# Attention into channel mixing on one core: values, differences and mixes in stretches of 512 columns

## The chip, the cores and the metric

One NeuronCore of a Trainium2 chip runs the whole program. The metric is device time in microseconds for one launch. Engines are named as in the profile: PE (TensorE's matmuls), PEld (its weight loads), DVE (VectorE), ACT (ScalarE), POOL (GpSimd), SP (SyncE). POOL issues the input loads, SP and ACT the stores.

## The reference, cut to what matters

There are 8 batches of 8 heads, 576 tokens, head dimension 64 and 32 memory slots. The model width is 8 x 64 = 512, the hidden width 1024.

```
a    = softmax(phi, axis=tokens)              # per batch, head and memory slot
k_m  = a.T @ k ;  v_m = a.T @ v               # 32 x 64 per head
x    = softmax(q @ k_m.T / 8) @ v_m           # 576 x 64 per head, heads side by side: 576 x 512
prev = x shifted by one token (zero first)
xk   = mu_k * x + (1 - mu_k) * prev
xr   = mu_r * x + (1 - mu_r) * prev
out  = sigmoid(xr @ w_r) * (relu(xk @ w_k)**2 @ w_v)
```

## The kernel before, in words

Everything between the loads and the stores stays on the chip, in bf16 with f32 accumulation. Tokens are the columns. A batch's 576 columns are nine blocks of 64 (QR): column 64 j + p holds token 9 p + j. The previous token of a column is therefore 64 columns to the left, except in block 0, where it is the last block, one column back.

The work is a list of steps, written out by hand as words in PLAN, and run in that order. Each step issues its instructions at once; each engine works through its own instructions strictly in the order of the plan, and waits only for the data and buffers that an instruction needs. PSUM has 8 banks; BANKS says which bank each new PSUM tile takes. The words used below:

- `b:exp`, `b:k`, `b:v`, `b:ko`, `b:kov`: exponential of phi (L255, ACT); matmul groups over the tokens that give keys, values and sums of the memory slots (L269, tile kvps). `b:zk`, `b:nk`/`b:ak`, `b:nv`/`b:av`: reciprocal of the sums; keys and values scaled, on DVE or ACT. `b:tk`/`b:ta`: transposing the keys.
- `b:q0`, `b:q1`: transposing q on DVE (L353). `b:s`: scores on PE and their exponentials on ACT (L368, L373).
- `b:fe`, `fs`, `fo` and `qe`, `qs`, `qo`: the softmax sums, folded and unfolded on DVE (L400 to L419). `b:y`, `b:w`: weights, exponential by reciprocal sum (L428, tile atn).
- `b:x0`, `b:x1`: the values of a batch, in its first 320 and its last 256 columns: 8 matmuls (L322, tile nops) and four copies from PSUM to the tile x (L440), all on ACT, or shared with DVE if the word ends in m.
- `b:d0d`, `b:d2d`: differences x - prev for two of the four 128-row parts (L452, L453). Three subtractions: two over whole blocks, one of 63 columns for block 0, and a copy for the first column.
- `b:k0d`, `b:r2e`, ...: mixes. The difference is scaled by mu - 1 (tile mu_d; on DVE at L465 if the word ends in d, on ACT at L463 if in e), and x added to it (L466), into xkT or xrT. These are rings of 4 batches (2304 columns).
- `c0:...` to `c8:...`: keys: 128 of 1024 hidden rows, times a stretch of columns: 4 matmuls (L576), the relu on ACT (L580), the square on DVE (L588), or on ACT if the word ends in s (L586). Stretch 0 is batch 0; stretches 1 to 8 have 512 columns each (the last 448), starting at column 576.
- `g:t`: the gate of 128 tokens: 4 matmuls (L609) and a tanh on ACT (L612). `o:t`: the product with w_v: 8 matmuls (L626), and the gating on DVE (L628), then the stores on SP.
- `0:mk`, `0:mr`: batch 0 alone mixes mu into v_m first (`nk`, `nr`: L474, tile vm), and lets the matmuls give xk and xr (L322, tile mxps, copied at L491).
- `busyNxM`: N matmuls of M x 128 columns on zeros (L214, tile idle). `p:...`: the loads on POOL's queue, of phi, k, v, q and the weights, each into one of two buffers.

Of the kernel before, what the change touches and what calls it, by code (L numbers as in the profile page):

```python
# [60 lines left out]
def kernel(  # L61
# [175 lines left out]

    def attention(b):
        st = {}
# [78 lines left out]
        def head_tiles(pss, src, lo, hi, cols=slice(0, None), **flags):  # L318
            for c in range(2):
                for g in range(HH):  # L320
                    r = slice(g * M, (g + 1) * M)
                    nc.tensor.matmul(pss[g][c * D:(c + 1) * D, cols], lhsT=src[r, c], rhs=st["at"][r, c, lo:hi],  # L322
                                     skip_group_check=True, **flags)
# [107 lines left out]
        def values(hf, both=False):  # L431

            def go():
                if "x" not in st:
                    st["x"] = own([128, ND, S], BF16, "x", 3)
                sl = HALVES[hf]
# [250 lines left out]
```

## Time and profile before

| | |
|---|---|
| three runs | 201.19, 201.27, 203.62 us; median 201.27 |
| profiled execution | 201.65 us, of which the span is 199.9 us |
| PE busy | 191.9 us (96%) |
| DVE busy | 151.3 us (76%) |
| ACT busy | 144.5 us (72%) |
| chain that ended last | PE 91%, ACT 4%, DVE 2% |
| DMA, mean over the span | 157 GB/s |
| TensorE's granted clock | 1.0 in all slices |

The span is the time from the first to the last recorded instruction; what the profiled execution took beyond it lies around it. Busy times of one group of instructions can be less than count times mean, since neighbours overlap. A line of the chain gives the start, the length and what ran; a line of a group gives count, busy time and mean, and then the idle time of the engine before it.

### The profile page before, as it was taken

Reading aid. Unit: us, or ns where it says so; the run is one execution under the profiler, and the core shown is the slowest. Engines: PE = TensorE matmul, PEld = TensorE weight load, DVE = VectorE, ACT = ScalarE, POOL = GpSimd, SP = SyncE. Lnnn points to the kernel's source line nnn. Section 1 sums busy time; section 2 is a strip of 40 time slices with the busy share of each in tenths; the row PEclk is TensorE's granted clock in tenths of the full one; section 3 lists DMA queues with packets and bytes.
Section 4 is the critical chain, followed back from the end, with each engine's and each line's share of the span. In section 5 each row is a group of like instructions: output and inputs, shape, how many; then the busy total and the mean of one; then the engine's idle time right before and its main releaser. Section 6 shows DMA issues by size and latency. Waiting matters only on the chain.

```text
span 199.9 us, 5381 instructions
## 1 busy us (share of the span) xinstructions
PE 191.9 (96%) x2148; PEld 99.6 (50%) x2170; DVE 151.3 (76%) x401; ACT 144.5 (72%) x311; POOL 29.7 (15%) x45
## 2 busy tenths in 40 slices
PE   8997999899999999999999999999999999999992
PEld 3474755585445445454457544444344444444451
DVE  5049698998689999999999999999997950031231
ACT  2236979648899998999799997876759868933210
POOL 7743142200143004070200000000000000000000
PEclk9999999999999999999999999999999999999999
DMA  6999999999999999999999421322422015014553
GB/s 160 191 261 209 205 208 198 268 214 293 233 218 230 286 259 281 206 240 224 207 253 190 106 56 35 71 54 54 99 62 52 2 41 119 0 38 101 116 117 105
DMA packets 24522, 31.30 MB, mean 157 GB/s; under 512 B 1960, under 2 KB 19632, under 8 KB 24496
## 3 DMA queue, kind: packets, MB, share of 16 engines
q0 software_dynamic: 17392, 20.91, 56.2%
q1 hardware_dynamic: 6336, 9.18, 18.4%
q10 hardware_dynamic: 768, 0.85, 1.3%
q8 instruction: 17, 0.28, 0.5%
q14 instruction: 9, 0.07, 0.1%
HBM read 38.28 MB, written 9.44 MB: 239 GB/s over the span
## 4 chain that ended last, share of the span: by engine, by line
PE 91%; ACT 4%; DVE 2%; issue 1%
PE pv L626 32%; PE pk L576 31%; PE pr L609 14%; PE idle L214 5%; PE kvps L269 4%; PE scps L368 2%; PE nops L322 2%; ACT sg L612 1%; PE mxps L322 1%; ACT e L373 1%; ACT L612 1%; DVE atn L428 1%; ACT rl L580 1%; PE ktps L335 1%; DVE lz L419 0%
## 5 line engine op out<-in xcount | busy, mean ns | idle before, releaser
L576 PE MATMUL pk<-xkT,wk 128*128 128x512 bf16 (+4 forms) x344 | 67.2, 340 | 0.4
L626 PE MATMUL pv<-wv,sq 128*128 128x512 bf16 (+1 forms) x320 | 65.6, 353 | 0.4
L580 ACT ACTIVATE rl<-pk 128x512 bf16<-128x512 f32 (+3 forms) x80 | 42.5, 552 | 13.1 <-PE pk L576 12.0
L576 PEld LDWEIGHTS <-wk 128*128 128x128 bf16 x352 | 33.0, 98 | 28.6 <-issue 1.4
L626 PEld LDWEIGHTS <-sq 128*128 128x128 bf16 x328 | 31.2, 98 | 29.0 <-issue 0.4
L609 PE MATMUL pr<-wr,xrT 128*128 128x512 bf16 x138 | 35.5, 380 | 0.3
L628 DVE SCALAR_TENSOR_TENSOR o<-sg,pv 128x512 f32<-128x512 f32 (+1 forms) x41 | 24.6, 615 | 13.7 <-PE pv L626 13.0
L612 ACT ACTIVATE sg<-pr 128x512 f32<-128x512 f32 x36 | 20.9, 594 | 13.6 <-PE pr L609 13.5
L588 DVE TENSOR_TENSOR sq<-rl 128x320 bf16<-128x320 bf16 (+5 forms) x55 | 15.8, 323 | 14.6 <-ACT rl L580 14.0
L586 ACT ACTIVATE sq<-rl 128x512 bf16<-128x512 bf16 (+5 forms) x49 | 24.5, 518 | 1.3
L463 ACT ACTIVATE mu_d<-diff,mu 128x576 bf16<-128x576 bf16 x30 | 21.4, 768 | 3.9 <-DVE diff L453 3.4
L609 PEld LDWEIGHTS <-xrT 128*128 128x128 bf16 x144 | 13.8, 98 | 15.6
L214 PE MATMUL idle<-zeros 128*128 128x512 bf16 (+3 forms) x74 | 13.6, 346 | 1.0 <-DVE zeros L143 1.0
L440 ACT CAST x<-nops 128x320 bf16<-128x320 f32 (+1 forms) x34 | 11.5, 420 | 2.9 <-PE nops L322 2.9
L466 DVE TENSOR_TENSOR xrT<-x,mu_d 128x1152 bf16<-128x1152 bf16 x14 | 10.5, 751 | 3.5 <-ACT mu_d L463 3.2
L428 DVE TENSOR_TENSOR atn<-e,lz 128x320 bf16<-128x320 bf16 (+2 forms) x31 | 12.9, 452 | 0.1
L452 DVE TENSOR_TENSOR diff<-x 128x512 bf16<-128x512 bf16 (+1 forms) x42 | 12.4, 352 | 0.4 <-ACT x L440 0.4
L353 DVE STREAM_TRANSPOSE qT<-q 128x576 uint32<-128x576 uint32 x16 | 11.9, 761 | 0.7 <-DMA q<-in_q_dram 0.7
L419 DVE STREAM_TRANSPOSE lz<-se 128x320 f32<-128x320 f32 (+3 forms) x21 | 11.9, 587 | 0.1
L373 ACT ACTIVATE e<-scps 128x288 bf16<-128x288 f32 x32 | 10.5, 421 | 1.7 <-PE scps L368 1.7
L255 ACT ACTIVATE em<-ph 128x1152 bf16<-128x1152 f32 (+1 forms) x9 | 9.4, 1060 | 2.6 <-DMA ph<-in_phi_dram 2.6
L410 DVE TENSOR_REDUCE se<-eT 128x18 f32<-128x576 bf16 (+3 forms) x15 | 10.9, 729 | 0.2
(68 smaller groups left out, 147.3 us busy)
## 6 DMA issues: line engine op xcount, KB each, us to landing
out_dram<-o SPq DMA_DIRECT2D x61, 128.0 KB, 2.4
...
kvs<-in_k_dram POOLq DMA_DIRECT2D x7, 576.0 KB, 16.9
q<-in_q_dram POOLq DMA_DIRECT2D x6, 576.0 KB, 12.6
...
```

The source lines that it names most:

```text
L214: nc.tensor.matmul(ps.rearrange("p (a b) -> p a b", b=128), lhsT=zeros, rhs=zeros.unsqueeze(1).to_broadcast([128, blocks, 128]), start=Tru ...
L373: nc.scalar.activation(e[:, hf], pss[c, hf], AF.Exp, scale=scale)
L428: nc.vector.tensor_mul(st["at"][:, c, sl], st["e"][:, c, sl], st["lz"][:, c, sl])
L463: nc.scalar.activation(t[:, i], st["d"][:, pr + i, :], AF.Copy, scale=mu1[:, o:o + 1])
L576: nc.tensor.matmul(pk[:, p0 - lo:p1 - lo], lhsT=wk_sb[:, di, fi * 128:(fi + 1) * 128], rhs=xk_T[:, di, p0 % RING:p0 % RING + p1 - p0], sta ...
L580: nc.scalar.activation(rl, pk, AF.Relu, scale=HALF_ROOT)
L586: nc.scalar.activation(sq[:, fi, p:p + p1 - p0], rl[:, part], AF.Square)
L588: nc.vector.tensor_mul(sq[:, fi, p:p + p1 - p0], rl[:, part], rl[:, part])
L609: nc.tensor.matmul(pr, lhsT=xr_T[:, di, c0:c0 + 128], rhs=wr_sb[:, di, :], start=(di == 0), stop=(di == ND - 1))
L612: nc.scalar.activation(gated[t], pr, AF.Tanh, scale=0.5)
L626: nc.tensor.matmul(pv[:, cols], lhsT=sq[:, fi, p:p + 128], rhs=wv_sb[:, fi, cols], start=(fi == 0), stop=(fi == NF - 1))
L628: nc.vector.scalar_tensor_tensor(o[:, cols], in0=gated[t][:, cols], scalar=1.0, in1=pv[:, cols], op0=AL.add, op1=AL.mult)
```

## The change

The steps `x0`/`x1`, `d` and `k`/`r` of batches 1 to 7 are no longer made per batch but per stretch of the 4032 columns of these batches: stretches x1 to x8, 512 columns each, the last 448. A batch's blocks are stored rotated by one: block 0 comes last in the ring (the stores take that into account), so that the mixes of a column need x at the same place and 64 columns ahead. The tile x of a stretch has 64 + 512 columns; its first 64 are copied on DVE from the tail of the stretch before.

A values step has four PSUM tiles of up to 512 columns; where a stretch contains the border of two batches, each batch's columns have their own matmuls. Only the first stretch makes its values in two pieces of 320 and 256. Differences are one subtraction over the stretch, and for a batch's end in it one of 63 columns and one copy. A mix is one addition over the stretch (two where the ring wraps), and one of 64 columns for a batch's end.

The tiles vb have four buffers instead of three. PLAN and BANKS are new throughout: words in another order, some steps by other engines (`ak` for `nk`, a key with s or without), fillers of other sizes, and loads in another order. Batch 3 takes its keys and values in two groups (`3:ko`, `3:v`).

```diff
 PLAN = [
-    "0:busy23x4 0:exp0 0:exp1 0:k0c 0:z p:k:0b p:q:00 p:q:01 0:k1c 0:busy16x3 0:ak 0:ta 0:q0 0:q1 0:mub 0:s1 0:s0",
-    "0:qe2 0:qe3 p:phi:1 p:v:0 0:busy25x1 0:fs1 0:qo2 0:qo3 1:exp 0:l0 0:v 0:h0z 0:y2 0:y3 0:l1 0:y0 0:nk0 0:nk1",
-    "0:busy10x2 0:h1z 0:y1 p:wk:4-8 0:nr1 0:mk0 0:mk1 c0:6a c0:7b p:wk:0-4 c0:5bs c0:7a c0:3bs p:k:1 0:nr0 c0:1b",
-    "c0:3a c0:2a c0:4b p:q:10 0:mr0 1:ko p:q:11 1:zk 1:nk c0:4a 1:q0 c0:6bs 1:q1 c0:1a 0:mu 1:ta 0:mr1 c0:0a 1:s0",
-    "1:s1 1:qe1 p:wr:0-4 1:qe0 1:fe1 c0:0bs p:v:1 c0:5as 1:fs0 c0:2bs 1:fs1 g:2 1:qo0 1:fo1 g:3 g:0 1:v 1:y0 1:qo1",
-    "1:y2 1:nv 1:y1 g:1 1:y3 1:x0m p:wv:0-2 1:x1m 1:d0d o:3a 1:d2d 1:k0d o:2a p:wv:2-4 o:1a 1:k2e o:0a o:3b o:1b",
-    "1:r0d p:phi:2 2:exp p:k:2 o:0b o:2b c1:3s 2:ko p:q:2 2:zk 2:ak 1:r2d c1:4s c1:6s 2:tk 2:q0 g:7 2:q1 c1:0 p:v:2",
-    "c1:5 2:s 2:qe2 2:qe3 2:qe1 2:fs1 2:qe0 2:fs0 2:qo2 2:y2 c1:7s g:6 2:fo0 2:v 2:qo3 p:phi:3 2:y0 c1:1s c1:2s g:5",
-    "2:av 2:y1 p:k:3 p:v:3 2:y3 3:exp g:4 o:5 2:x0m g:8 2:x1m 3:kov p:q:3 3:zk 2:d2d 2:d0d 3:ak 3:q1 3:av o:7 2:k2e",
-    "3:tk p:v:4 3:q0 2:k0e o:6 o:4 2:r2e 3:s 3:fe0 c2:1s 2:r0d c2:7 c2:2s 3:fe1 3:fs c2:6 p:q:4 c2:3s 3:fo0 3:fo1",
-    "p:phi:4 g:11 g:9 3:y0 p:k:4 3:y3 4:exp p:k:5 3:y1 3:y2 c2:5 p:phi:5 c2:4 c2:0 g:12 3:x1m 4:kov 3:x0m 4:zk 3:d0d",
-    "4:ak 3:d2d 4:av o:8 3:k0e 4:q1 p:phi:6 4:q0 3:k2e g:10 p:v:5 5:exp 4:tk o:10 3:r0d o:11 c3:0 5:kov p:q:5 5:zk",
-    "3:r2e 4:s c3:1s p:phi:7 4:qe0 4:qe1 4:fe1 4:fs 5:ak p:k:7 c3:3 4:qo3 c3:5 4:y3 4:fo0 5:q0 7:exp g:13 5:nv 6:exp",
-    "4:qo2 4:y1 c3:4 4:y2 5:ta c3:7 5:q1 o:9 c3:2s c3:6 4:y0 g:15 p:v:7 4:x1m o:13 4:x0 4:d0d 7:kov 5:s 7:zk1 7:zk0",
-    "4:d2d 5:qe1 5:qe0 5:qe2 7:ak 5:qe3 4:k0d 4:k2e 5:fs 5:fo 4:r0e p:q:6 o:15 o:12 6:q0 g:16 7:av c4:3s 5:y2 p:k:6",
-    "c4:2 p:q:7 g:17 c4:6s 7:q0 7:q1 4:r2e p:v:6 c4:7 7:ta c4:5 c4:4 5:w0 5:y3 g:14 c4:0 c4:1 7:s o:14 6:q1 5:x1",
-    "6:kov 6:zk 7:fe0 5:x0 7:qs0 6:nk g:20 6:av 7:fe1 g:18 5:d0d 5:r0d 5:d2d o:16 7:qs1 5:k0e 5:k2e g:19 5:r2d 7:qo0",
-    "7:qo1 6:ta o:17 7:fs1 o:18 c5:0 6:s 6:fe1 6:fe0 6:qs3 c5:2s 6:qs0 6:qo3 6:qs1 c5:3s 6:fo0 6:qs2 g:21 6:qo2 6:y1",
-    "6:y2 6:y3 c5:7s c5:5s 6:y0 c5:6 7:y0 o:19 7:qo2 c5:4s 7:y2 c5:1s g:23 g:24 7:y1 6:x1m o:23 g:22 7:qo3 6:x0m",
-    "6:d0d 7:y3 o:20 6:d2d 7:x0m 6:k0e 6:k2d o:22 7:x1m 7:d0d o:21 g:26 c6:4s c6:1s 7:d2d c6:2s 7:k0d 7:k2d c6:5s",
-    "7:r0e 6:r0d c6:3 g:25 c6:0 c6:6 c7:3 c6:7 c7:0s 6:r2d c7:1s 7:r2e c7:7s o:25 o:24 o:26 c8:6 g:27 c7:6s c8:2 g:28",
-    "c8:5s c8:3s c8:0s g:31 c7:5s c8:4 c8:1s c7:2s g:32 c7:4 o:27 o:28 c8:7s g:29 o:31 g:30 o:30 o:32 g:34 g:33 o:33",
-    "o:29 g:35 o:34 o:35",
+    "0:busy3x2 0:busy22x2 0:busy13x4 0:exp1 p:k:0b 0:exp0 0:k0c 0:mu 0:z 0:k1c p:q:01 0:ak 0:q1 0:hc0 p:q:00 0:q0",
+    "0:ht1 0:mub 0:s0 0:s1 0:qe2 0:qe3 0:busy3x1 p:v:0 0:busy3x1 0:fs1 0:l1 0:v 0:nk0 0:nr0 0:l0 0:h0z p:phi:1 0:qo2",
+    "p:wk:4-8 0:nr1 0:busy16x2 0:qo3 0:nk1 p:k:1 0:y2 0:y3 0:h1z 0:y1 0:y0 0:mk1 0:mk0 1:exp c0:4bs 0:mr1 c0:6b 1:ko",
+    "p:wk:0-4 c0:6a p:q:11 1:zk c0:5a 1:ak c0:4a c0:2a p:q:10 1:q1 c0:3b c0:7bs 1:q0 1:ta 0:mr0 c0:2b c0:5b c0:3a",
+    "1:s1 1:fe1 p:wr:0-4 1:s0 p:v:1 1:qe0 1:qe1 c0:7a c0:0a 1:fs1 1:fs0 1:qo0 1:qo1 c0:1b c0:1as g:0 c0:0bs 1:fo1",
+    "1:y2 g:2 1:v p:wv:0-2 1:y0 1:av 1:y1 g:1 1:y3 g:3 x1:v0 o:3a x1:v1m x1:d0d p:wv:2-4 x1:d2d o:2a x1:k0d p:phi:2",
+    "x1:k2d o:1a 2:exp o:1b p:k:2 o:2b x1:r0d o:3b o:0a o:0b 2:ko 2:zk0 2:zk1 p:q:2 x1:r2d 2:q0 c1:3 2:ak 2:q1 c1:5",
+    "c1:0s p:v:2 c1:1 2:tk c1:4 c1:2 2:s 2:qe0 2:v 2:qe2 c1:6s p:phi:3 g:4 g:7 2:qe3 p:k:3 2:qs2 2:qs3 2:qo2 2:qe1",
+    "p:q:3 2:qo3 2:fs0 2:fo0 3:exp 2:y3 g:6 2:y1 2:y0 c1:7s g:5 2:av 2:y2 o:7 x2:v 3:q0 3:ko 3:zk 3:ak x2:d0d x2:d2d",
+    "3:q1 x2:k0e o:6 o:4 x2:k2e 3:ta x2:r2e x2:r0d o:5 p:v:3 3:s p:phi:5 3:fe0 3:v c2:1 c2:6s p:q:4 3:fe1 3:fs 5:exp",
+    "p:phi:4 c2:2 3:qo1 p:v:5 p:v:4 c2:4s 3:nv c2:3 3:qo0 3:qo2 3:y1 3:y2 3:qo3 g:9 p:k:4 c2:0 c2:5s 3:y3 3:y0 g:8",
+    "g:11 4:q0 c2:7 g:10 4:q1 x3:v x3:d0d x3:d2d x3:k2d 4:exp x3:k0e o:11 o:8 o:10 4:kov 4:zk p:k:5 x3:r2e x3:r0e",
+    "4:ak 5:kov p:q:5 p:phi:7 4:av 5:zk0 5:zk1 5:nk c3:6 5:q0 p:v:7 c3:2 4:ta o:9 p:k:7 p:phi:6 4:s 4:qe1 4:fe1 4:qe0",
+    "c3:4 4:fs 5:q1 c3:1 4:fo0 4:qo2 c3:7 7:exp 4:qo3 5:ta 4:y2 5:av p:q:6 4:y3 p:q:7 4:y0 4:y1 g:12 g:14 c3:3 p:v:6",
+    "c3:0 c3:5 5:s 7:kov x4:v 5:qe0 5:qe2 g:15 x4:d0d x4:d2d x4:k2d x4:k0e g:13 o:13 p:k:6 7:zk0 7:zk1 5:qe3 x4:r0e",
+    "7:ak 5:qe1 o:15 x4:r2e o:12 c4:4 5:fs c4:0 c4:2 7:av c4:5 6:exp 5:fo1 c4:1s 5:fo0 7:ta c4:6s 5:y2 5:y0 o:14 g:18",
+    "x5:v 7:q1 7:q0 x5:d0d 5:y1 6:kov x5:d2d 6:zk g:19 6:q1 c4:3 7:s 6:q0 c4:7s x5:k2d 6:nv g:16 7:qe1 x5:k0e g:17",
+    "x5:r0d 7:qs1 o:18 x5:r2e 5:y3 7:qe0 o:17 7:qe2 7:qe3 6:ak c5:5 c5:7s 6:ta c5:4s 7:fs1 o:16 6:s 7:qo3 7:qs0 6:qe2",
+    "6:fe0 6:qe3 6:qs0 6:qs1 g:21 6:qs2 6:fo0 6:qo2 c5:3 7:qo0 c5:1 6:y2 6:y0 7:qo2 g:23 6:qs3 7:y2 g:22 6:y1 c5:2s",
+    "c5:0s 6:qo3 6:y3 c5:6s 7:y3 o:19 x6:v x6:d0d o:23 7:y0 x6:d2d x6:k0d x6:k2e o:22 o:21 x7:v g:20 o:20 c6:5 x7:d0d",
+    "7:qo1 x6:r0e c6:2 x6:r2d c6:3 c6:0s c6:7 x7:k0e x7:d2d c6:1s c6:4 c6:6s 7:y1 g:26 g:27 g:25 o:27 x7:k2d x7:r0e",
+    "x7:r2d x8:v x8:d0d x8:d2d o:25 o:26 c7:1 g:31 g:24 x8:r2d x8:k2e c7:0 c7:2 c7:3 c7:7s c7:5s g:30 x8:k0d o:24",
+    "c7:6s c7:4s x8:r0d g:28 c8:3 c8:4 o:28 c8:7 c8:0s o:31 c8:2 g:33 o:30 g:34 c8:6s c8:5 c8:1s g:32 g:29 o:32 o:33",
+    "g:35 o:29 o:34 o:35",
 ]
...
+    states = [{} for _ in range(B)]
+
+    def head_tiles(pss, st, src, lo, hi, cols=slice(0, None), **flags):
+        for c in range(2):
+            for g in range(HH):
+                r = slice(g * M, (g + 1) * M)
+                nc.tensor.matmul(pss[g][c * D:(c + 1) * D, cols], lhsT=src[r, c], rhs=st["at"][r, c, lo:hi],
+                                 skip_group_check=True, **flags)
+
     def attention(b):
-        st = {}
+        st = states[b]
...
-                vb = own([128, 2, D], BF16, "vb", 3)
+                vb = own([128, 2, D], BF16, "vb", 4)
...
-        def values(hf, both=False):
-        def diff(pr, n=1):
-        def mix(which, pr, n=1, by_act=False):
...
+    TOK = (B - 1) * S
+    xs, ds = {}, {}
+    def chunk_x(c):
+        lo = (c - 1) * CT
+        hi = min(lo + CT, TOK)
+        n, plain = hi - lo, min(hi, TOK - QR) - lo
+        ends = [b * S - QR for b in range(1, B) if lo <= b * S - QR < hi]
+        def tile_x():
+            if c not in xs:
+                xs[c] = work.tile([128, ND, QR + CT], BF16, name="x", tag=f"x{c % 3}")
+            return xs[c]
+        def values(c0, c1, both=False):
+            def go():
+                x = tile_x()
+                if c > 1:
+                    nc.vector.tensor_copy(x[:, :, :QR], xs[c - 1][:, :, CT:])
+                pss = [psum.tile([128, CT], F32, name="nops", tag=bank())[:, :c1 - c0] for _ in range(ND)]
+                for b in range(1, B):
+                    g0, g1 = max(lo + c0, (b - 1) * S), min(lo + c1, b * S)
+                    if g0 < g1:
+                        head_tiles(pss, states[b], states[b]["vb"], g0 - (b - 1) * S, g1 - (b - 1) * S,
+                                   slice(g0 - lo - c0, g1 - lo - c0), start=True, stop=True)
+                for i in range(ND):
+                    (nc.vector.tensor_copy if both and i % 2 else nc.scalar.copy)(x[:, i, c0:c1], pss[i])
+            return go
+        def diff(pr, m):
+            def go():
+                if c not in ds:
+                    ds[c] = work.tile([128, ND, CT], BF16, name="diff", tag=f"diff{c % 2}")
+                x, d = xs[c][:, pr:pr + m], ds[c][:, pr:pr + m]
+                nc.vector.tensor_sub(d[:, :, :plain], x[:, :, QR:QR + plain], x[:, :, :plain])
+                for e in ends:
+                    e -= lo
+                    first = xs[c - 1][:, pr:pr + m, e:e + QR]
+                    nc.vector.tensor_sub(d[:, :, e + 1:e + QR], first[:, :, 1:], x[:, :, e:e + QR - 1])
+                    nc.vector.tensor_copy(d[:, :, e:e + 1], first[:, :, :1])
+            return go
+        def mix(which, pr, m, by_act=False):
+            def go():
+                ring = (xk_T, xr_T)[which][:, pr:pr + m]
+                t = work.tile([128, 2, CT], BF16, name="mu_d", tag=turn("mu_d", 2))[:, :m]
+                for i in range(m):
+                    o = which * ND + pr + i
+                    if by_act:
+                        nc.scalar.activation(t[:, i, :n], ds[c][:, pr + i, :n], AF.Copy, scale=mu1[:, o:o + 1])
+                    else:
+                        nc.vector.tensor_scalar_mul(t[:, i, :n], ds[c][:, pr + i, :n], mu1[:, o:o + 1])
+                x = xs[c][:, pr:pr + m]
+                cut = -(S + lo) % RING
+                for p0, p1 in ((0, cut), (cut, plain)) if 0 < cut < plain else ((0, plain),):
+                    g = (S + lo + p0) % RING
+                    nc.vector.tensor_add(ring[:, :, g:g + p1 - p0], x[:, :, QR + p0:QR + p1], t[:, :, p0:p1])
+                for e in ends:
+                    e -= lo
+                    g = (S + lo + e) % RING
+                    nc.vector.tensor_add(ring[:, :, g:g + QR], xs[c - 1][:, pr:pr + m, e:e + QR], t[:, :, e:e + QR])
+            return go
+        return values, diff, mix
+    def chunk_steps(c):
+        values, diff, mix = chunk_x(c)
+        n = min(CT, TOK - QR - (c - 1) * CT)
+        spans = {"0": (0, 5 * QR), "1": (5 * QR, S)} if c == 1 else {"": (QR, QR + n)}
+        steps = {}
+        for w, (c0, c1) in spans.items():
+            steps[f"v{w}"] = values(c0, c1)
+            steps[f"v{w}m"] = values(c0, c1, True)
+        steps["dd"] = diff(0, ND)
+        for i in (0, 2):
+            steps[f"d{i}d"] = diff(i, 2)
+            for w in range(2):
+                steps[f"{'kr'[w]}{i}d"] = mix(w, i, 2)
+                steps[f"{'kr'[w]}{i}e"] = mix(w, i, 2, by_act=True)
+        return steps
...
             j, p0 = divmod(r, QR)
+            j = (j + 1) % NJ if b else j
...
+    chunks = {f"x{c}": chunk_steps(c) for c in range(1, len(STARTS))}
...
+        elif who in chunks:
+            todo.append((n, -1, word, chunks[who][name]))
```

More of the change, by code (lines that the diff above doesn't have):

```diff
@@ L316, in norm_v @@
             return go
[L318 to L323, printed above, removed]
         def reload():
@@ L429, in weigh @@
             return go
-        def values(hf, both=False):
[L433 to L436, printed above, removed]
-                pss = [half_tile(hf, "nops") for _ in range(ND)]
-                head_tiles(pss, st["vb"], sl.start, sl.stop, start=True, stop=True)
-                for i in range(ND):
-                    (nc.vector.tensor_copy if both and i % 2 else nc.scalar.copy)(st["x"][:, i, sl], pss[i])
-            return go
-        before = [[(QR, 5 * QR, 0), (1, QR, S - QR)], [(5 * QR, S, 4 * QR)]]
-        def diff(pr, n=1):
-            def go():
-                if "d" not in st:
-                    st["d"] = own([128, ND, S], BF16, "diff", 2)
-                x, d = st["x"][:, pr:pr + n], st["d"][:, pr:pr + n]
-                for lo, hi, p0 in before[1] + before[0]:
-                    nc.vector.tensor_sub(d[:, :, lo:hi], x[:, :, lo:hi], x[:, :, p0:p0 + hi - lo])
-                nc.vector.tensor_copy(d[:, :, 0:1], x[:, :, 0:1])
-            return go
-        def mix(which, pr, n=1, by_act=False):
-            def go():
-                dst = (xk_T, xr_T)[which][:, pr:pr + n, x0:x0 + S]
-                t = work.tile([128, 2, S], BF16, name="mu_d", tag=turn("mu_d", 2))[:, :n]
-                for i in range(n):
-                    o = which * ND + pr + i
-                    if by_act:
-                        nc.scalar.activation(t[:, i], st["d"][:, pr + i, :], AF.Copy, scale=mu1[:, o:o + 1])
-                    else:
-                        nc.vector.tensor_scalar_mul(t[:, i], st["d"][:, pr + i, :], mu1[:, o:o + 1])
-                nc.vector.tensor_add(dst, st["x"][:, pr:pr + n], t)
-            return go
+        before = [[(QR, 5 * QR, 0), (1, QR, S - QR)], [(5 * QR, S, 4 * QR)]]
         def norm_mu(w, c):
@@ L484, in go @@
                 vm = st["vm", w]
-                head_tiles(pss, vm[:, 0], lo, hi, start=True, stop=False)
+                head_tiles(pss, st, vm[:, 0], lo, hi, start=True, stop=False)
                 for n, (c0, c1, p0) in enumerate(before[hf]):
-                    head_tiles(pss, vm[:, 1], p0, p0 + c1 - c0, slice(c0 - lo, c1 - lo),
+                    head_tiles(pss, st, vm[:, 1], p0, p0 + c1 - c0, slice(c0 - lo, c1 - lo),
                                start=False, stop=n == len(before[hf]) - 1)
@@ L524, in attention @@
             steps[f"y{i}"] = weigh(i // 2, half)
-            steps[f"d{i}"] = diff(i)
-            for w in range(2):
-                steps[f"{'kr'[w]}{i}"] = mix(w, i)
         for i in range(2):
@@ L531, in attention @@
             steps[f"w{i}"] = weigh(i)
-            steps[f"d{2 * i}d"] = diff(2 * i, 2)
-            for w in range(2):
-                steps[f"{'kr'[w]}{2 * i}d"] = mix(w, 2 * i, 2)
-                steps[f"{'kr'[w]}{2 * i}e"] = mix(w, 2 * i, 2, by_act=True)
-        steps["dd"] = diff(0, 4)
         for hf in range(2):
-            steps[f"x{hf}"] = values(hf)
-            steps[f"x{hf}m"] = values(hf, both=True)
             for w in range(2):
```

6 lines of the change are left out of this document (3 added, 3 removed).

## The prediction

> **What bounds the kernel now.** I read the page's shares and slices first, then the busy time in stretches, then the chain that ended last, then the groups by form.
>
> ```profile
> PE 191.9 (96%) x2148; PEld 99.6 (50%) x2170; DVE 151.3 (76%) x401; ACT 144.5 (72%) x311; POOL 29.7 (15%) x45
> PE   8997999899999999999999999999999999999992
> DVE  5049698998689999999999999999997950031231
> ACT  2236979648899998999799997876759868933210
> ```
>
> TensorE is busy from end to end. VectorE is nearly full too from slice 8 to slice 30 and nearly empty in the last nine; the share of 76% hides that.
>
> ```profile
> 20.00:25.00 5.00, 5.00 (x60) 3.71 (x66) 3.00 (x10) 4.56 (x14) 0.83 (x2) 1.00 1.21 205
> 25.00:30.00 5.00, 4.63 (x163) 2.90 (x147) 4.91 (x16) 3.84 (x11) 2.15 (x3) 1.00 1.23 208
> 35.00:40.00 5.00, 4.49 (x42) 2.95 (x43) 5.00 (x18) 3.34 (x9) 1.48 (x2) 1.00 1.23 267
> 44.70:120.00 75.30, 74.62 (x1052) 38.17 (x1064) 71.11 (x187) 68.78 (x153) 11.95 (x16) 1.00 1.03 219
> 120.00:196.00 76.00, 75.63 (x414) 34.85 (x419) 47.56 (x119) 48.84 (x96) 0.00 (x0) 1.00 0.28 63
> ```
>
> The first figure after the length is TensorE's busy time, then weight loads, VectorE, ScalarE. From 44.7 to 196 us TensorE misses 1.05 us of 151.3. What can still be won lies ahead of 44.7.
>
> ```profile
> 18.63 0.88 PE mxps L322 x20
> 20.39 4.52 PE pk L576 x36
> 46.26 0.32 PE pk L576
> 146.78 4.32 PE pk L576 x20
> 196.05 0.42 DVE o L628
> ```
>
> In the chain (start, length, what) the keys begin at 20.3, and the end is the last product's gating at 196.05. VectorE's queue shows that it is just in time, not idle:
>
> ```profile
> 145.60 0.76 DVE L466 TENSOR_TENSOR xkT<-x,mu_d 128x1152 bf16<-128x1152 bf16 x1
> ```
>
> This addition ends at 146.36 and feeds the keys that start at 146.78.
>
> **How I add.** Every word of the plan gets its row's price. On TensorE a 512-column matmul takes 0.216 (4.32 for 20), so a key or a gate costs 0.86 and a product 1.73; a kov group is 0.87, ko 0.78, v 0.75, a score group 0.48, a values group 0.24 (256 columns) to 0.27 (320). On the other engines these rows hold (count | busy us, mean ns):
>
> ```profile
> L440 ACT CAST x<-nops 128x320 bf16<-128x320 f32 x18 | 6.7, 446 | 2.5 <-PE nops L322 2.5
> L440 DVE CAST x<-nops 128x320 bf16<-128x320 f32 x10 | 4.4, 485 | 0.2 <-PE nops L322 0.2
> L466 DVE TENSOR_TENSOR xkT<-x,mu_d 128x1152 bf16<-128x1152 bf16 x14 | 10.3, 747 | 0.2
> L452 DVE TENSOR_TENSOR diff<-x 128x512 bf16<-128x512 bf16 x28 | 10.5, 417 | 0.4 <-ACT x L440 0.4
> L452 DVE TENSOR_TENSOR diff<-x 128x126 bf16<-128x126 bf16 x14 | 3.1, 221 | 0.0
> ```
>
> Between 126 and 1152 elements VectorE's bf16 operations lie on 0.14 + 0.00053 per element: 0.68 for 1024, 0.21 for 128. Neighbours overlap: from the start of batch 1's first xr mix (44.14) to the end of batch 6's second xk mix (146.36) the rows add to 113 us and the clock says 102.2. So a full VectorE queue takes 0.90 of its rows.
>
> **The change, part by part.** *TensorE.* The values stay 14 groups, because the stretches that straddle a batch are cut in two: 3.6 us before and after. Batch 3's kov becomes ko and v: 0.78 + 0.75 - 0.87 = +0.66. Keys, gates, products, scores: the same counts.
>
> *PSUM copies of the values* fall from 56 to 36, all but two on ScalarE. VectorE loses 22 (12 x 0.417 + 10 x 0.485 = 9.9) and keeps 0.8; it gains seven copies of 4 x 64 columns, which no row shows: between 0.17 (the two-element copy) and 0.29 (kmT, 256 from PSUM); I take 0.25 as nearer in size, 1.8. Net -7.3. ScalarE goes from 14.3 to 18.8: 24 copies of 512 at 0.60 (the row of rl, same size from PSUM), the rest smaller. +4.5.
>
> *Differences:* 14 x 0.68, 2 x 0.55, 14 x 0.22, 14 x 0.17: 16.1 against 16.0.
>
> *Mixes:* now 28 x 0.75 + 26 x 0.37 = 30.6. After: 24 additions of 2 x 512 (16.4), four cut by the ring (3.3), four of 2 x 384 (2.2), 28 edge additions of 2 x 64 (5.9), 32 scalings at 0.33 or 0.29 (10.3): 38.1. +7.5.
>
> *Squares* change engine in the new order: VectorE +4.6, ScalarE -7.0. Folds, weights and small copies: VectorE +0.3, ScalarE +0.6.
>
> Sum: VectorE +5.1 by rows, 4.6 at 0.90; ScalarE -1.9. TensorE waits for neither unless a stage runs short, so I go by stages.
>
> *To the first key.* The fillers grow from 11,776 to 13,056 columns, so kvps begin near 9.4, not 8.93. The 16 fillers that held the key transposes until 12.6 are gone, and the transposes run in two halves; scores then wait for the second q load and its turn (11.38 + 0.78 = 12.2, against 13.45), if the swapped q halves land in the same slots. But head group 1's exponentials now come second (0.66), so the fold begins at 14.0 instead of 14.7, and four vm products (4 x 0.34) stand ahead of the weights in VectorE's queue: 13 rows, 5.65 x 0.90 = 5.1, to 19.1; the first mix (0.3) and two copies (0.8) give the first key at 20.2 to 20.3, as now. I take 0, bounds -0.5 and +0.8.
>
> The Trainium skill (TensorE: Matmul & The Clock Gate, Part 1) has the clock double after some 3.4 us of sustained matmuls, at a point that varies from run to run; here the fillers start 0.43 apart until 6.9 and faster then. By that rule an early switch, 2 us sooner, would end the fillers 1 us sooner; the sum would be 1 us less.
>
> *First key to the first c1 key and 2:ko.* TensorE's words add to 23.8 before and took 46.26 - 20.32 = 25.9: 2.1 lost. After, they add to 23.6 (the mu transpose has moved ahead). ScalarE decides: its rows from the first mix copies to the last value copy of batch 1 add to 19.4 and took 18.9 with 1.9 of it idle, so 0.875 of the rows; after, phi 1's exponential moves in (1.17), with 0.56 for vb and 0.9 for more copies, less squares: 21.8 x 0.875 = 19.1, ending at 38.6 against 38.4. Then d0d, d2d, one product, k0d, k2d on VectorE (4.5 x 0.9 = 4.0) are done at 42.6, ahead of the key that needs them at 44 or later. wk's first half (15.1 us from issue to landing, at 21.9) is now queued behind k 1 (0.59 MB, some 2.8 us); its first reader stands at 24.1, so it may wait half a us. I take 1.7 lost, bounds 0.5 and 4; the first c1 key then starts at 20.3 + 22.8 + 1.7 = 44.8.
>
> *From there to the end.* 148.3 before took 196.05 - 46.26 = 149.8 (loss 1.5); after 149.0 + 1.5. Where VectorE could be late: from x1's second xk mix (42.6) to x5:k0e its rows add to 87.3, 78.6 at 0.90: 121.2. TensorE from the first c1 key (44.8) to c5:5 holds 32 keys (27.7), 16 gates (13.8), 14 products (24.2), kv groups (5.8), scores, transposes and values (4.8): 76.3, with its loss 77.0: 121.8. Slack 0.6; at c6:5 it is 0.4 (143.9 against 144.3). (At c2:1, c3:6 and c4:4 the slack is 1 to 2 us.) I take 0.6, bounds 0 and 4. If it is late, the keys queue behind it, and squares and products after them. Stretches 7 and 8 have 15 us between values and keys, so nothing is exposed there. The end, two half products and their stores, is as now.
>
> Sum against the profiled execution (201.65, span 199.9): 0 - 0.2 (the moved transpose) - 0.4 (2.1 to 1.7) + 0.7 + 0.6 = +0.7, 202.4. Its median stands 0.4 lower (201.27): 202.0.
>
> **The rivals.** (a) *Nothing is lost on the way:* early loss 0.5, no late mix. -0.2 - 1.6 + 0.7 = -1.1, 200.2 as a median. For it: the stages after 44.7 already run without a hole, and ScalarE gets lighter. Against: mixes and kvps share the start with the same loads.
>
> (b) *VectorE becomes the bound* at c5:5 and c6:5, slower. It decides from the point where its rows run over 0.90; each per cent over 113 us of rows is 1.0 us, and 5% gives 5.1 less the slack of 0.4, in place of my 0.6: 206.1. For it: hardly any slack by the sum, 28 edge additions. Against: TensorE's 1.05 us of idle shows the old queue, just as tight, holding.
>
> (b') *No overlap at all.* If neighbours on VectorE no longer overlapped, 87.3 instead of 78.6 would put x5:k0e 8.7 later, 8.1 past the slack: some 209.5. Against: the old queue did 113 us of rows in 102.2. The Trainium skill (VectorE: DVE Perf Modes, "The DRAIN you can't avoid") has this as its rule, that the next operation does not start until the pipe is empty, and advises fewer operations, where this change has 436 for 401. By that rule, (b').
>
> (c) *Loads late:* v 5 now stands in POOL's queue ahead of v 4 and k 4 and waits for batch 3's v group at 65; k 4 issues at 67. With the median landing of 16.9 it comes at 84, needed at 81.8: +2.2, 204.2. Against: by then the queue has drained, and four loads of 0.59 MB at 219 GB/s need 11 us.
>
> (d) *The new form buys nothing because TensorE never waited for the copies.* That is in the forecast: 20 copies fewer, none on its path.
>
> **How the numbers follow.** Forecast 0.50 (its own range 200.8 to 203.5), (a) 0.27, (b) 0.14, (c) 0.06, (b') 0.03. 2% is 4.0 us, about what a measurement of this kernel can tell from no change. (b) passes it for 0.11, (c) for 0.01, (b') for 0.03: slower 0.15. Faster by 2% needs all of (a) and 2.9 us more, from the first stage alone: 0.03. The rest, 0.82, is within. The range takes in (a), 0.4 below it for the first key, and (b) up to its 5%: 199.8 to 206.0.
>
> **What would show it.** First key near 20.3, first c1 key at 44 to 45, VectorE's busy time up by 4 to 6 us, ScalarE's down by about 2, TensorE's idle after 45 us under 2 us: right. A hole in TensorE ahead of c5:5 or c6:5 that ends with a VectorE addition: (b). A hole that ends with a DMA near 82: (c). Wrong altogether: a first key before 18 or after 22, or a change over 4 us with no such hole.

## The result, and the profile after

The changed kernel takes 202.53 us (median of 20 runs, 201.72 to 203.19), the kernel before 201.22 us in the same sessions (20 runs): a ratio of 1.0054, with an interval of 1.0034 to 1.0073. (Each ratio here is taken over the executions in the faster of two states alone, so it can differ by up to 0.3% from the quotient of the two medians beside it.) That is slower by 0.5%, so no difference by the bound of 2% and just outside the scatter. The prediction was 202.0 us. The profiled execution took 202.22 us with a span of 200.4; before it was 201.65 and 199.9.

The page after, busy shares and the rows of 40 slices:

```profile
PE 190.3 (95%) x2210; PEld 101.1 (50%) x2230; DVE 156.7 (78%) x436; ACT 143.9 (72%) x305; POOL 29.7 (15%) x45
PE   8969899999999999999899999999999999999992
DVE  5158689899889999989799999999998797431231
ACT  3242999718989899869889998876699777745410
```

VectorE has 5.4 us more to do, ScalarE 0.6 us less. TensorE's row shows a new notch at slice 20, about 95 us, where it showed nines before. The stretches (length, then busy time of TensorE, weight loads, VectorE, ScalarE and POOL, then TensorE's granted clock, DMA share and GB/s):

```profile
10.00:15.00 5.00, 3.07 (x47) 1.78 (x47) 2.87 (x7) 2.44 (x8) 1.45 (x2) 0.71 1.17 262
15.00:20.00 5.00, 4.75 (x129) 3.49 (x129) 4.45 (x14) 1.36 (x4) 2.27 (x3) 0.61 1.22 211
44.40:120.00 75.60, 73.66 (x1044) 37.93 (x1055) 70.74 (x198) 66.81 (x142) 11.93 (x16) 1.00 1.03 219
120.00:196.60 76.60, 76.11 (x425) 35.24 (x430) 54.07 (x150) 51.44 (x100) 0.00 (x0) 1.00 0.28 63
```

Between 44.4 and 120 us TensorE now misses 1.94 us; before it missed 0.68 in the like stretch. Behind 120 it misses 0.49, against 0.37. So the loss lies between 44 and 120, not where VectorE was feared. Its places, in TensorE's timeline (start, length, engine, line, what; in brackets the idle time before it and what ended it):

```profile
83.08 0.94 PE L279 MATMUL kvps<-kvs,em 64*32 64x192 bf16 x72 [0.26 <-DMA kvs<-in_k_dram]
97.01 0.94 PE L279 MATMUL kvps<-kvs,em 64*32 64x192 bf16 x72 [0.94 <-ACT e L376]
122.79 1.89 PE L617 MATMUL pk<-xkT,wk 128*128 128x512 bf16 x8
145.05 5.13 PE L617 MATMUL pk<-xkT,wk 128*128 128x512 bf16 x23
```

The first two lines are 5:kov and 7:kov, the groups that start batches 5 and 7; they waited 0.26 and 0.94 us. The last two are the first keys of stretches 5 and 6, and they waited for nothing. From the chain that ended last:

```profile
19.46 0.41 PE mxps L245 x16
44.40 0.32 PE pk L617
...
68.41 14.54 DMA kvs<-in_k_dram
83.08 0.94 PE kvps L279 x72
```

The chain runs through k 5's load: issued at 68.41, landed 14.54 us later at 82.95, and 5:kov starts at 83.08.

The books against the profile before: the first key at 20.28 (20.32 before); the first c1 key and 2:ko done at 45.3 (46.26), which is 1.0 us won; from there to TensorE's end 151.3 us (149.8), 1.5 us lost. Waits are 1.3 of these (TensorE idle for 2.37 us there, before for 1.08), and the two holes are 1.2 of the 1.3. TensorE's work is only 0.2 us more. The split of batch 3's group does show, with 0.9 us more of k and v matmuls (6.40 against 5.48), but the 96 values matmuls fall by as much (2.99 against 3.94): a stretch that straddles a batch runs its 16 as one block of 0.42 us, where two words of 8 took 0.34 and 0.32 before.

The 1.0 us won up to 45.3 is one execution against one. Eight profiled executions have the same code up to 58 us (this one and those of numbers 1 and 5 to 10 below). In them the first key starts between 19.9 and 21.1 us (median 20.6) and the first c1 key between 44.1 and 45.4 (median 44.7), so the median won is nearer to 0.6.

### The profile page after: what moved, and what is told of

Its sections match the earlier page's. It is cut to its first block, busy times and chain, and to the rows that moved or that the text cites. A ratio compares the mean times of both kernels' runs of the same rounds, so it can differ in the third digit from the quotient of the medians.

```text
span 200.4 us, 5541 instructions
## 1 busy us (share of the span) xinstructions
PE 190.3 (95%) x2210; PEld 101.1 (50%) x2230; DVE 156.7 (78%) x436; ACT 143.9 (72%) x305; POOL 29.7 (15%) x45
## 4 chain that ended last, share of the span: by engine, by line
PE 79%; DMA 13%; POOL 2%; ACT 2%; issue 2%; DVE 0%; POOLq 0%
PE pv L667 29%; PE pk L617 28%; PE pr L650 14%; DMA kvs<-in_k_dram 7%; DMA kvs<-in_v_dram 5%; PE kvps L279 4%; PE idle L215 2%; PE scps L371 1%; PE nops L245 1%; POOL kvs L126 1%; POOL q L182 1%; ACT xkT L458 1%; POOL kvs L129 1%; ACT em L265 1%; PE mxps L245 0%
## 5 line engine op out<-in xcount | busy, mean ns | idle before, releaser
L621 ACT ACTIVATE rl<-pk 128x512 bf16<-128x512 f32 (+3 forms) x80 | 42.6, 558 | 15.7 <-PE pk L617 14.8
L629 DVE TENSOR_TENSOR sq<-rl 128x320 bf16<-128x320 bf16 (+3 forms) x67 | 19.8, 326 | 9.3 <-ACT rl L621 8.8
L560 ACT ACTIVATE mu_d<-diff,mu 128x512 bf16<-128x512 bf16 (+1 forms) x32 | 21.1, 723 | 5.0 <-DVE diff L550 3.3
L627 ACT ACTIVATE sq<-rl 128x512 bf16<-128x512 bf16 (+5 forms) x37 | 17.5, 496 | 0.9
L536 ACT CAST x<-nops 128x512 bf16<-128x512 f32 (+3 forms) x34 | 15.9, 566 | 1.6 <-PE nops L245 1.6
L279 PE MATMUL kvps<-kvs,em 64*32 64x64 bf16 (+2 forms) x864 | 10.6, 221 | 2.6 <-DMA kvs<-in_v_dram 1.0
L356 DVE STREAM_TRANSPOSE qT<-q 128x576 uint32<-128x576 uint32 x16 | 12.2, 766 | 1.1 <-DMA q<-in_q_dram 1.1
L431 DVE TENSOR_TENSOR atn<-e,lz 128x320 bf16<-128x320 bf16 (+1 forms) x32 | 12.7, 443 | 0.1
L215 PE MATMUL idle<-zeros 128*128 128x256 bf16 (+2 forms) x60 | 11.8, 379 | 1.0 <-DVE zeros L144 1.0
L422 DVE STREAM_TRANSPOSE lz<-se 128x320 f32<-128x320 f32 (+2 forms) x24 | 12.5, 536 | 0.1
L279 PEld LDWEIGHTS <-em 64*32 64x32 bf16 x864 | 8.7, 91 | 6.1 <-issue 3.8
L545 DVE TENSOR_TENSOR diff<-x 128x1024 bf16<-128x1024 bf16 (+1 forms) x16 | 10.6, 666 | 1.4 <-ACT x L536 1.0
## 6 DMA issues: line engine op xcount, KB each, us to landing
q<-in_q_dram POOLq DMA_DIRECT2D x4, 288.0 KB, 12.4
```

The source lines that it names most:

```text
L215: nc.tensor.matmul(ps.rearrange("p (a b) -> p a b", b=128), lhsT=zeros, rhs=zeros.unsqueeze(1).to_broadcast([128, blocks, 128]), start=Tru ...
L279: nc.tensor.matmul(kvps[c][g * M:(g + 1) * M], lhsT=em[ROWS[c], j, g, :], rhs=kvs[ROWS[c], at, g, j, :], start=j == 0, stop=j == NJ - 1, s ...
L536: (nc.vector.tensor_copy if both and i % 2 else nc.scalar.copy)(x[:, i, c0:c1], pss[i])
L560: nc.scalar.activation(t[:, i, :n], ds[c][:, pr + i, :n], AF.Copy, scale=mu1[:, o:o + 1])
L621: nc.scalar.activation(rl, pk, AF.Relu, scale=HALF_ROOT)
L627: nc.scalar.activation(sq[:, fi, p:p + p1 - p0], rl[:, part], AF.Square)
```

## The experiments

My theory was that TensorE sets the time and that the 1.5 us are waits for loads of k, the prediction's rival (c) at another place. The rivals: VectorE's added work (b), and ScalarE, which the profile names at 97.01.

**1. The loads in the old order.** k 4 and k 5 stood behind v 5 in POOL's queue, and v 5 waits for its buffer until batch 3's v group is done.

```diff
-    ... p:v:5 p:v:4 ... p:k:4 ... p:k:5 ...
+    ... p:v:4 p:k:4 p:k:5 p:v:5 ...
```

> The changed kernel with one edit: the loads of batch 4's v and k and batch 5's k stand ahead of batch 5's v in POOL's queue, instead of behind it. Nothing else moves. Theory (loads): batch 5's v waits for batch 3's v group at 66 us and holds the other three back; the load queue runs nearly dry, so 5:kov waits 0.3 us at 83 and 7:kov 0.95 us at 96. Then the four issue from 58 us on, k 5 lands near 77, and both holes go or shrink: 0.8 to 1.3 us less than the changed kernel (ratio to before about 0.999). Rival (ScalarE): the hole at 96 is a PSUM bank that ScalarE's exponentials of batch 5 hold, as the wait names them; then at most the 0.3 us at 83 goes (ratio about 1.004).

Measured: 202.30 us against 201.40, ratio 1.0033 (1.0008 to 1.0058). TensorE's timeline:

```profile
82.94 1.70 PE L279 MATMUL kvps<-kvs,em 64*32 64x192 bf16 x144
97.65 0.94 PE L279 MATMUL kvps<-kvs,em 64*32 64x192 bf16 x72 [1.39 <-DMA kvs<-in_k_dram]
```

4:kov and 5:kov run as one block of 144 matmuls: the first hole is gone. The second stays, and here the profile names k 7's load, not ScalarE. That load cannot start before 5:kov has ended, because it goes into the buffer that 5:kov reads.

**2. Two loads less.** The loads of v 4 and v 5 are left out.

```diff
-    ... p:v:5 p:v:4 ...
```

> The changed kernel without the loads of v for batches 4 and 5 (these batches use the v of batches 2 and 3 that still lie in the buffers; the values are not the reference's). Two of 36 loads fewer, 1.2 MB, and nothing in POOL's queue waits for batch 3's v group. Theory (loads): k 5 and k 7 land 5 us earlier, both holes go: 1.0 to 1.4 us less than the changed kernel (ratio to before 0.998). Rival (ScalarE's bank): the hole at 96 stays, at most 0.3 us less (ratio 1.004).

Measured: 202.07 us against 201.40, ratio 1.0021 (1.0001 to 1.0041). Emptier queues bring about as much as the better order, with intervals that overlap each other's; no line of a profile stands behind this run, so it says no more.

**3. Batch 3 in one group again**, to take back the 0.66 us.

```diff
-    ... 3:ko ... p:v:3 ... 3:v ... 3:nv
+    ... p:v:3 3:kov ... 3:nv
```

> The changed kernel with batch 3's keys and values in one group again (3:kov for 3:ko and 3:v, its v load ahead of it, and its vb scaled right after). Step of the sum: +0.66 us of TensorE work. If TensorE is the only bound there: 0.6 us less than the changed kernel (ratio 1.002). If the loads bound the stage up to 97 us, part of it returns as a longer wait at 83 and 96: but batch 5's v no longer waits for a later v group, so its load issues some 6 us earlier, and the holes should shrink too: 0.6 to 1.8 us less (ratio 0.996 to 1.002). A change under 0.2 us would speak against the step.

Measured: 205.12 us, ratio 1.0165 (1.0131 to 1.0198), some 2 us slower than the changed kernel. My expectations missed it. In TensorE's timeline, and in the stretch around it:

```profile
61.63 1.64 PE L279 MATMUL kvps<-kvs,em 64*32 64x192 bf16 x72 [2.40 <-DMA kvs<-in_v_dram]
```

```profile
60.00:65.00 5.00, 3.37 (x78) 2.00 (x79) 1.78 (x6) 1.98 (x5) 1.37 (x2) 0.66 1.14 285
```

The group waits 2.40 us for v 3, issued at 38.6 and landed at 61.4 in the changed kernel too. It then runs 1.64 us in place of 0.94, and the clock of that stretch is 0.66. The split has a reason that I had not seen: only the v part needs v 3, and it stands behind three products.

**4. More fillers at the start**, to keep the clock up between 10 and 20 us.

```diff
-    ... 0:mub 0:s0 ... 0:l1 ... 0:busy16x2
+    ... 0:mub 0:busy7x2 0:s0 ... 0:l1 0:busy7x2 ... 0:busy26x2
```

> The changed kernel with more filler matmuls in the first 20 us: 7 of 256 columns ahead of batch 0's scores, 7 after the first softmax sum, 26 for 16 ahead of the mixes, so that TensorE has no gap from 11.4 to 19 us. In the changed kernel its granted clock is 0.71 in 10 to 15 us and 0.61 in 15 to 20. Theory A (the low clock costs): with the clock at 1.0 the first scores take 0.45 us as before the change, not 0.9, the fold starts 0.3 to 0.4 us earlier, the first key stands near 19.9, and the whole is 0.3 us less (ratio 1.004). Rival B: batch 0's v load (15.25 us) and VectorE set the first mix anyway, and the clock costs nothing: within 0.1 us of the changed kernel. Rival C: the fillers themselves delay the scores or the softmax sum: up to 0.5 us more.

Measured: 205.51 us, ratio 1.0189 (1.0152 to 1.0226). One stretch and two lines of the timeline:

```profile
15.00:20.00 5.00, 4.91 (x131) 3.91 (x136) 4.60 (x14) 1.34 (x4) 2.19 (x3) 1.00 1.21 217
```

```profile
87.28 0.26 PE L279 MATMUL kvps<-kvs,em 64*32 64x192 bf16 x2 [2.02 <-issue]
...
101.13 0.94 PE L279 MATMUL kvps<-kvs,em 64*32 64x192 bf16 x72 [1.98 <-DMA kvs<-in_k_dram]
```

The clock is full from 15 us on, where it was 0.61, and yet the first key stands at 20.50, within the 19.9 to 21.1 of the eight executions above: the clock in these 5 us brings no gain at the first key. What made the kernel slower lies later. From the first key to the first c1 key it takes 25.2 us, against 24.0 to 24.6 in the eight, with 0.60 us of waiting for VectorE at batch 1's scores (29.10) and a stop of 0.68 us within 1:v (35.26). Then 5:kov stops for 2.02 us two matmuls short of its end, again waiting for nothing that the profile shows, and k 7's load, which waits for 5:kov, is late by as much. Why the fillers bring this about is not shown; the last section says what such stops have in common.

**5. and 6. 7:kov moved back**, once with the loads reordered and once alone. If it only waits for its load, 2.3 us of other work ahead of it covers that.

```diff
-    ... 5:s 7:kov x4:v 5:qe0 5:qe2 g:15 ...
+    ... 5:s x4:v 5:qe0 5:qe2 g:15 7:kov ...
```

> Kernel: the changed one with (i) the loads of v 4, k 4 and k 5 put ahead of v 5 and (ii) TensorE's step 7:kov moved two value and gate groups later (behind x4:v and g:15, 2.3 us of TensorE work). Theory (the loss after 45 us is TensorE waiting for loads of k at 5:kov and at 7:kov): both holes close, 0.3 + 1.0 to 1.4 us come back, time about 201.2, ratio to the kernel before 0.998 to 1.001, and 7:kov shows no wait over 0.3 us. Rival 1 (7:kov waited for ScalarE and its PSUM bank): the wait moves along with the step and stays near 1 us, ratio about 1.003 as with the reordered loads alone. Rival 2 (the time is given by VectorE's chain, not by these holes): the holes close, others of the same size open between 100 and 150 us, ratio 1.003 to 1.006.

> Kernel: the changed one with only 7:kov moved behind x4:v and g:15. Theory of the loads: the hole at 5:kov (0.3 us) stays, that at 7:kov (0.9 us) closes, time about 201.6, ratio to the kernel before 1.001 to 1.003. If the hole at 7:kov is not the load's, nothing is gained: ratio 1.004 to 1.006.

Measured: with the loads 201.69 us against 201.26, ratio 1.0002 (0.9974 to 1.0031); alone 202.61, ratio 1.0041 (1.0008 to 1.0075). The first looks like the theory; the second lies in the range that I had given for the case that the hole is not the load's, but its interval takes in the theory's 1.001 to 1.003 as well. The timeline decides. In the run with the loads:

```profile
95.22 1.36 PE L245 MATMUL nops<-atn,vb 32*64 32x128 bf16 x16
...
97.48 0.94 PE L279 MATMUL kvps<-kvs,em 64*32 64x192 bf16 x72
```

7:kov shows no wait. But x4:v, the values group now ahead of it, takes 1.36 us; in the changed kernel it takes 0.42. The 0.94 us have moved into it. From the start of 5:s to the product behind these groups it is 4.41 us in both runs, and 4.38 in the changed kernel: nothing was won. By the list of banks x4:v writes to banks 2, 0, 4 and 6; c3:5 had filled bank 0, and 5:s banks 4 and 6, and ScalarE, busy without a break from 91.3 to 97.5 us in the changed kernel, empties them. In the run with the loads x4:v's matmuls start bank by bank at 95.22, 95.56, 95.86 and 96.17 us. The last three stand 0.05 us behind the end of c3:5's relu (95.51) and of the first two exponentials of 5:s (95.82 and 96.11). So x4:v, moved ahead, waits for ScalarE's emptying of its banks.

That does not make ScalarE a cause of the hole in the changed kernel. There 7:kov writes to banks 5 and 7, both emptied by 95.05, and starts at 97.01, 0.13 us behind the landing of k 7 (issued at 85.17, landed at 96.88); 5:kov stands as far behind its load (82.95 and 83.08). The "ACT e" that the profile names for 7:kov empties none of its banks: it is the update nearest in time, an exponential that ended at 96.90. The hole at 7:kov is the load's alone, as my theory had it, and moving 7:kov back uncovered a second wait that happens to be as long. With k 7 in time and the order kept, 7:kov's own 0.94 us would have lain over that second wait; no run has that.

**7. VectorE lighter.** The additions on the 64 columns at a batch's end, where the main addition has written them already, are left out (24 of 28).

```diff
                 for e in ends:
+                    if e - lo < plain:
+                        continue
```

> Kernel: the changed one that leaves out the additions over the 64 columns at a batch's end where the main addition has already written those columns (the ring then holds the main addition's values there), some 5 us less on VectorE. Theory (TensorE and its loads set the end, VectorE keeps up): not more than 0.3 us faster than the changed kernel, ratio to the kernel before 1.003 to 1.006, the holes at 5:kov and 7:kov as they were. Rival (b) of the prediction (VectorE's added work is the loss): about 1.2 us come back, ratio 0.998 to 1.001.

Measured: 203.00 us, ratio 1.0060 (1.0025 to 1.0095), with 152.5 us on VectorE. 4.2 us less work there bring nothing; 5:kov waited 0.66 and 7:kov 1.61 us in its profile, both for loads of k. Outside the holes nothing is won either: from x4:v to TensorE's end it is 98.66 us, against 98.71. Rival (b) is out as the cause of the loss.

**8. VectorE heavier.** The same additions are done twice.

```diff
+                    nc.vector.tensor_add(ring[:, :, g:g + QR], xs[c - 1][:, pr:pr + m, e:e + QR], t[:, :, e:e + QR])
```

> Kernel: the changed one that does each addition over the 64 columns at a batch's end twice: some 6 us more on VectorE, spread over seven batches. Theory: my sum leaves VectorE 0.4 to 0.6 us of lead at the first keys of stretches 5 and 6, so about 4 us of the added time by then shows there: 205 to 206, ratio 1.018 to 1.025, with TensorE's holes ending on VectorE's additions at the keys of stretches 5 and 6. Rival (VectorE has several us of slack after 45 us because the loads and TensorE hold it up): under 0.6 us slower than the changed kernel, ratio 1.004 to 1.009.

Measured: 206.23 us, ratio 1.0220 (1.0172 to 1.0268), with 162.5 us on VectorE. The size is as my sum had it: 5.8 us of work cost 3 to 4 us. The place isn't. In the timeline:

```profile
77.86 0.40 PE L245 MATMUL nops<-atn,vb 32*64 32x448 bf16 x8 [0.85 <-DVE atn L431]
...
115.47 0.34 PE L245 MATMUL nops<-atn,vb 32*64 32x320 bf16 x8 [0.79 <-DVE atn L431]
```

TensorE waits for VectorE at values groups, whose weights come last in VectorE's queue, and besides 0.48 us at a gate, 0.29 at a product and only 0.20 at a key. VectorE keeps up in the changed kernel, with little to spare.

**9. and 10. Both waits covered.** A gate group that needs neither k 7 nor ScalarE's exponentials goes ahead of both. It takes bank 5, empty since 94.6 us; banks 3 and 5 are exchanged from there on.

```diff
-    ... 5:s 7:kov x4:v 5:qe0 5:qe2 g:15 ...
+    ... 5:s g:15 x4:v 7:kov 5:qe0 5:qe2 ...
```

> Kernel: the changed one with the loads of v 4, k 4 and k 5 ahead of v 5, and at 95 us TensorE's order 5:s, g:15, x4:v, 7:kov in place of 5:s, 7:kov, x4:v, g:15; from there the PSUM banks 3 and 5 are exchanged, so that g:15 takes a bank that was read out at 94.6 us. Theory now: two things come late at the same place, k 7 (lands at 96.8) and ScalarE's exponentials of 5:s (which give x4:v its banks at about 96.9), so putting either step first only moves the 0.94 us; 1.73 us of gate work that waits for neither covers both. The hole goes: 0.9 us less than with 7:kov merely moved back, 200.8 us, ratio to the kernel before 0.994 to 0.998, 7:kov and x4:v without a wait over 0.2 us (x4:v 0.42 us long, not 1.36). Rival (ScalarE itself is behind by about a microsecond there, so whatever is covered here comes back at the next step that needs it, x4:v's copies and the keys of stretch 4): another hole of 0.5 to 0.9 us by 115 us, ratio 0.999 to 1.002.

> Kernel: the changed one with only TensorE's order 5:s, g:15, x4:v, 7:kov (banks 3 and 5 exchanged from there on), loads as they were. Theory (two late things at 7:kov, and apart from them k 5's load at 5:kov): 0.9 us faster than the changed kernel, 201.6, ratio to the kernel before 0.999 to 1.003, the hole of about 0.3 us at 5:kov still there. Rival (ScalarE's backlog comes back later): ratio 1.003 to 1.006.

Measured: with the loads reordered 201.30 us against 201.29, ratio 1.0001 (0.9978 to 1.0025); alone 201.94, ratio 1.0028 (1.0006 to 1.0049). The timeline of the first, then of the second:

```profile
96.40 0.42 PE L245 MATMUL nops<-atn,vb 32*64 32x128 bf16 x16
97.08 0.94 PE L279 MATMUL kvps<-kvs,em 64*32 64x192 bf16 x72 [0.25 <-DMA kvs<-in_k_dram]
```

```profile
96.67 0.94 PE L279 MATMUL kvps<-kvs,em 64*32 64x192 bf16 x72
...
112.22 0.34 PE L245 MATMUL nops<-atn,vb 32*64 32x320 bf16 x8 [0.30 <-DVE atn L431]
```

x4:v is back at 0.42 us. From 5:s to the product it is now 3.80 and 3.48 us, against 4.38: 0.58 and 0.90 won. From there to the end of 6:kov it is 14.62 and 14.95, against 14.51: 0.11 and 0.44 given back, in the second run within x5:v, whose second eight matmuls wait 0.30 us for VectorE. Net 0.47 and 0.46. So the hole closes, but for 0.25 us in the first run, and about half a microsecond of it is kept in each of the two traces. The new hole behind it that my rival foretold shows in the second run alone. The ratios do not tell number 9 (1.0001) from number 5 (1.0002). With the loads in order the kernel stands where the kernel before stood, and no better.

**11. Batch 3's group whole, with v 3 loaded ahead of q 3**, on top of number 9; the turns of q 3 on VectorE move behind stretch 2's differences.

```diff
-    ... p:q:3 ... x2:v 3:q0 3:ko ... x2:d2d 3:q1 ... p:v:3 ... 3:v ... 3:nv
+    ... p:v:3 p:q:3 ... x2:v 3:kov ... x2:d2d 3:q0 3:q1 3:nv ...
```

> Kernel: that with the loads reordered and the gate group ahead of x4:v and 7:kov, and besides batch 3's keys and values again in one group (3:kov), with v 3's load put ahead of q 3's and the two turns of q 3 moved behind the differences of stretch 2 on VectorE. Theory (the split of batch 3's group is only the answer to v 3's load landing at 61.4 us): v 3 lands where q 3 did, at about 58.5 us, 3:kov starts without a wait over 0.3 us; TensorE has 0.74 us less to do, but the additions for the keys of stretch 2 end half a microsecond later, so 0.2 to 0.7 us come back: 200.6 to 201.1, ratio to the kernel before 0.996 to 0.999. Rival (VectorE decides at the keys of stretch 2, and the turns of q 3, now waiting until 61.4, push its additions): a hole of over 0.7 us that ends with a VectorE addition ahead of the keys of stretch 2 at 65 us, ratio 1.000 to 1.004.

Measured: 201.58 us against 201.37, ratio 1.0011 (0.9995 to 1.0028). TensorE's timeline:

```profile
58.27 0.94 PE L279 MATMUL kvps<-kvs,em 64*32 64x192 bf16 x72
...
65.31 0.59 PE L617 MATMUL pk<-xkT,wk 128*128 128x512 bf16 x2 [0.29 <-DVE o L669]
66.17 4.04 PE L617 MATMUL pk<-xkT,wk 128*128 128x512 bf16 x18 [0.27 <-DVE xkT L571]
```

v 3 lands at 58.2 and the whole group runs without a wait, as the theory had it. But the keys of stretch 2, which now come sooner, wait twice for VectorE, 0.56 us in all. The 0.66 us of the split are work on TensorE that lies in a gap it would have anyway.

One measure is free of the scatter of the first 45 us: the time from the start of 2:ko and the first c1 key, whichever comes first, to TensorE's end, in one profiled execution of each kernel.

| kernel | us |
|---|---|
| before | 151.5 |
| changed | 153.1 |
| 1, loads in the old order | 152.7 |
| 6, 7:kov moved back | 152.8 |
| 5, both of these | 152.1 |
| 10, gate group ahead | 152.2 |
| 9, gate group ahead and loads in the old order | 151.7 |
| 11, number 9 with batch 3 whole | 151.8 |
| 7, VectorE lighter | 153.5 |
| 8, VectorE heavier | 156.1 |

The change loses 1.6 us here, and number 9 brings 1.4 of them back. Of that, 0.4 is a group of scores at 87.62 us that took 0.92 us in the profile after and 0.53 in number 9, which no edit explains; the rest is the two holes.

## Why the prediction came out as it did

**The first key** (0, bounds -0.5 and +0.8): 20.28 against 20.32, and 20.6 as the median of the eight executions, all within the bounds. On the way two steps were off. I had scores at 12.2 and the fold at 14.0; they came at 12.40 and 14.49, because the scores took 0.91 us in place of 0.50 before, behind a hole of 0.94 us: the granted clock was 1.00 from 11 to 12 us, 0.54 from 12 to 13 and 0.50 from 13 to 18. The Trainium skill (TensorE: Matmul & The Clock Gate, Part 1) has TensorE fall to half its clock after an idle window of some 3.4 us; by the trace here 0.94 us at 11.5 us, behind a thin stretch, and 2.40 us at 59 us (number 3) were enough to bring it down (to 0.66 over the 5 us behind the second), while 1.98 us at 99 us (number 4) left the clock at 1.00. The rival made of that page, an early full clock worth 1 us, did not come: number 4 has the clock and not the gain.

**First key to first c1 key** (1.7 lost, bounds 0.5 and 4): 1.4 lost (1.4 to 1.6 in seven of the eight executions, 1.9 in the other). ScalarE's last value copies of batch 1 ended at 38.41 (38.6 predicted), the second xk mix at 42.30 (42.6), the first c1 key started at 44.40 (44.8). No wait for wk's first half shows.

**The terms.** VectorE +5.4 (+5.1). ScalarE -0.6 (-1.9): copies +4.4 and squares -7.0 came as summed (+4.5 and -7.0), but the copies of the key means, kbd and kmT, add 1.4 for which I had 0.6. The new rows:

```profile
L536 ACT CAST x<-nops 128x512 bf16<-128x512 f32 x24 | 12.3, 600 | 1.6 <-PE nops L245 1.6
L567 DVE TENSOR_TENSOR xkT<-x,mu_d 128x1024 bf16<-128x1024 bf16 x12 | 8.2, 686 | 0.2
L571 DVE TENSOR_TENSOR xkT<-x,mu_d 128x128 bf16<-128x128 bf16 x14 | 3.1, 222 | 0.3
```

0.60, 0.686 and 0.222 us, where I took 0.60 from the row of rl and 0.68 and 0.21 from the line through the old sizes.

**The step that failed: 0.6 for late mixes at c5:5 and c6:5.** The VectorE sum was good. It put the end of x5:k0e at 121.2 and the key at 121.8. They came at 122.34 and 122.79, both a microsecond later, so 0.45 us ahead in place of 0.6; at c6:5 0.49 in place of 0.4. By a slack of that size nothing is lost, and I charged 0.6. Rivals (b) and (b') fall with it: without any overlap of neighbours x5:k0e would have ended near 130.

**In its place stood rival (c), at other steps.** I had v 5 in front of k 4 and k 4 landing at 84, 16.9 us after its issue. k 4 took 12.4 us, landed at 80.1 and was in time for 81.88. k 5, behind it in the same queue, landed at 82.95 and cost 0.26 us; and k 7, which I had not followed at all, cost 0.94. The Trainium skill (DMA: Bandwidth & Descriptors, Two DMAs through the same engine are not ordered) says that within one queue of one DMA engine descriptors start in order. The trace agrees: v 5, v 4, k 4 and k 5, issued at 66.21, 66.95, 67.67 and 68.41, landed in that order, at 73.7, 77.2, 80.1 and 82.95.

**The sum** had +0.7 for the profiled execution, and +0.57 came. That it came so near is luck, since several terms were off and cancelled. The split's 0.66 came as 0.9 of k and v matmuls, and the values matmuls, which I had equal before and after, fell by 0.95, so that the work grew by 0.2 in place of 0.7. The 0.6 of VectorE was not lost. The waits that came in its place, 1.2 us of loads, were not in the sum. The early stage lost 0.7 less than before where I had 0.4 less. And the profiled execution after has an early first key among the eight (20.28; median 20.6). The medians carry no such accident and stand 1.3 apart, where I had +0.7 as well. Rival (a), nothing lost on the way, would have needed the holes at 83 and 96 closed. Number 9 closes most of them and stands at 1.0001, so the 1.1 us that this rival promised are not there even then; its interval leaves room for less than half of them.
